# First token chunk of an attention and SwiGLU kernel: scores of both head groups for its first half ahead, first two wide products by halves of 256 tokens

## The chip, the cores and the metric

The kernel runs on one core of one Trainium2 chip. The metric is device time in microseconds (us) of that core, the median over several executions. Every kernel was timed in turn with the kernel before on the same chip. All profiled executions were of the undisturbed (fast) state, so fast runs are compared with fast runs throughout.

## The reference

Attention with projected keys and values (8 batches, 8 heads, 1024 tokens, head dimension 64; keys and values are projected from 1024 tokens to 64 by E and F), followed by a SwiGLU feed-forward network on the 8192 tokens of width 512, with an inner width of 1536:

```python
k_proj = np.einsum('ks,bhsd->bhkd', E, k)
v_proj = np.einsum('ks,bhsd->bhkd', F, v)
scores = scale * np.matmul(q, k_proj.transpose(0, 1, 3, 2))
scores = scores - np.max(scores, axis=-1, keepdims=True)
attn = np.exp(scores)
attn = attn / (np.sum(attn, axis=-1, keepdims=True) + 1e-09)
x = np.matmul(attn, v_proj)            # then [b, h, s, d] -> [b*s, h*d]
# ...
g = x @ w_gate
silu = g * (1.0 / (1.0 + np.exp(-g)))
val = x @ w_val
out = silu * val @ w_out
```

## The kernel before

The kernel works through 16 chunks of 512 tokens (two to a batch). For each chunk and each of 12 feature tiles of 128 it runs a gate block (`f_g`: four products of 128x512, summed over d_model) and a value block (`f_v`). The attention of later batches and the output products are slipped between these blocks by hand. Only the first chunk has nothing to hide behind, and all of this case is about it. Its attention is cut in four blocks `u`: head group `g` (heads 0-3 or 4-7) and token half `i` (256 tokens), with `g, i = divmod(u, 2)`. So `u` = 0, 1 is group 0, both halves, and `u` = 2, 3 is group 1.

The steps of a block, cut to their cores:

```python
def u_T(b, u, at, eng):   # transposes the queries of the block: 4 transposes, one copy (qT)
def u_S(b, u, at):        # scores: 4 products with BD (projected keys), Exp on ScalarE -> ee
def u_R(b, u):            # VectorE: row sums (zz) and reciprocal (rr)
def u_N(b, u):            # normalization, ee * rr -> AA
    # ...
    eng = nc.vector if b == 0 and u in (1, 3) else nc.gpsimd
def u_A(b, u, eng):       # 4 transposes of AA into a bank of the pool ps_a (3 banks), copy -> AT
def u_PV(b, ch, pr, eng): # one product of 512 tokens for a pair of heads, copy -> xT
def u_KV(b, what, hs, at):# projection of the keys or values of heads hs: 8 products (256 columns);
                          # for values, two copies into BDV:
    # ...
            eng = nc.vector if b or h0 else nc.scalar

def f_g(c, f):
    ps = ps_g.tile([P, CW], FP32, name="gps", tag="gps")      # ps_g has 2 banks
    x = xT[divmod(c, CH)]
    for kt in range(NKT):
        nc.tensor.matmul(out=ps[:], lhsT=wg[:, kt, f * P : (f + 1) * P], rhs=x[:, kt, :],
                         start=(kt == 0), stop=(kt == NKT - 1))
    th = fw.tile([P, CW], FP32, name="th", tag="th")
    nc.scalar.activation(out=th[:], in_=ps[:], func=AF.Tanh, scale=0.5)
    gp[0] = (ps, th)
```

The order of the opening; `warm(n)` issues n products of zeros (fillers) that are meant to keep the matrix engine's clock up:

```python
        warm(8)
        turn(0)
        turn(1)
        warm(6)
        u_KV(0, "k", (0, 4), at="y")
        # ... warm, key transposes, the other key half, warm ...
        u_T(0, 0, "a", nc.scalar)
        u_T(0, 1, "a", nc.scalar)
        warm(2)
        u_S(0, 0, "g")
        u_S(0, 1, "g")
        u_T(0, 2, "a", nc.scalar)
        u_T(0, 3, "a", nc.scalar)
        u_R(0, 0); u_N(0, 0); u_R(0, 1); u_N(0, 1)     # four lines in the kernel
        load_w_gv(4, 6, (0,))
        warm(3)
        u_S(0, 2, "g")
        u_S(0, 3, "g")
        for u in (2, 3):
            u_R(0, u)
            u_N(0, u)
        # ... loads ...
        warm(3)
        u_A(0, 0, nc.scalar)
        u_KV(0, "v", (0, 4), at="y")
        u_A(0, 1, nc.scalar)
        u_PV(0, 0, 0, nc.vector)
        u_PV(0, 0, 1, nc.vector)
        warm(3)
        u_A(0, 2, nc.scalar)
        u_KV(0, "v", (4, 8), at="y")
        u_A(0, 3, nc.scalar)
        u_PV(0, 0, 2, nc.scalar)
        u_PV(0, 0, 3, nc.vector)
        # ... then the stream: f_g, f_v of each feature tile ...
```

The softmax here doesn't subtract the row's maximum and nothing guards it: scores larger than these inputs give would overflow.

Of the kernel before, what the change touches and what calls it, by code (L numbers as in the profile page):

```python
# [12 lines left out]
BF16 = mybir.dt.bfloat16  # L13
# [9 lines left out]
P = 128  # L23
NJ = S // P
NPAIR = H // 2
NKT = DM // P
# [8 lines left out]
def kernel(  # L35
# [98 lines left out]
    def copy(eng, out, in_):  # L134
        (nc.scalar.copy if eng is nc.scalar else eng.tensor_copy)(out=out, in_=in_)  # L135

    def u_KV(b, what="kv", hs=(0, H), at="a"):
# [20 lines left out]
        if "v" in what:  # L158
            tv = t[64:128].rearrange("p (a c) d -> p a c d", c=2)
            ps = slice(h0 // 2, h1 // 2)  # L160
            eng = nc.vector if b or h0 else nc.scalar
            copy(eng, BDV[b % 2][0:64, ps, 0:64], tv[:, ps, 0, :])
            copy(eng, BDV[b % 2][64:128, ps, 64:128], tv[:, ps, 1, :])
# [83 lines left out]
    def u_N(b, u):  # L247
# [6 lines left out]
        else:  # L254
            a = AA[b, u] = aw.tile([P, 2, 4, KP], BF16, name="AA", tag="AA", bufs=4)
            a = a[:]
        eng = nc.vector if b == 0 and u in (1, 3) else nc.gpsimd
        eng.tensor_tensor(  # L258
# [22 lines left out]
    def u_PV(b, ch, pr, eng=nc.scalar):  # L281
# [10 lines left out]
        copy(eng, xT[b, ch][:, pr, :], ps[:])  # L292


    gp = {}

    def f_g(c, f):
        ps = ps_g.tile([P, CW], FP32, name="gps", tag="gps")
        x = xT[divmod(c, CH)]
        for kt in range(NKT):  # L300
            nc.tensor.matmul(  # L301
                out=ps[:],
                lhsT=wg[:, kt, f * P : (f + 1) * P],
                rhs=x[:, kt, :],
                start=(kt == 0),
                stop=(kt == NKT - 1),
            )
        th = fw.tile([P, CW], FP32, name="th", tag="th")
        nc.scalar.activation(out=th[:], in_=ps[:], func=AF.Tanh, scale=0.5)  # L309
        gp[0] = (ps, th)  # L310

    def f_v(c, f):
        ps = ps_v.tile([P, CW], FP32, name="vps", tag="vps")
        x = xT[divmod(c, CH)]
        for kt in range(NKT):
            nc.tensor.matmul(  # L316
                out=ps[:],
                lhsT=wv[:, kt, f * P : (f + 1) * P],
                rhs=x[:, kt, :],
                start=(kt == 0),  # L320
                stop=(kt == NKT - 1),
            )
        g, th = gp.pop(0)
# [74 lines left out]
    with tc.manual_schedule():  # L398
# [45 lines left out]
        turn(1)  # L444
        warm(6)
        u_KV(0, "k", (0, 4), at="y")
        warm(2)
        u_KT(0, at="v", prs=(0, 2))
        warm(3)
        u_KV(0, "k", (4, 8), at="y")  # L450
        warm(2)
        u_KT(0, at="v", prs=(2, 4))
        u_T(0, 0, "a", nc.scalar)
        u_T(0, 1, "a", nc.scalar)
        warm(2)
        u_S(0, 0, "g")
        u_S(0, 1, "g")
        u_T(0, 2, "a", nc.scalar)
        u_T(0, 3, "a", nc.scalar)
        u_R(0, 0)  # L460
        u_N(0, 0)
        u_R(0, 1)
        u_N(0, 1)
        load_w_gv(4, 6, (0,))
        warm(3)
        u_S(0, 2, "g")
        u_S(0, 3, "g")
        for u in (2, 3):
            u_R(0, u)
            u_N(0, u)  # L470
        load_w_gv(4, 6, (1,))
# [6 lines left out]
        load_k(1)  # L478
        warm(3)
        u_A(0, 0, nc.scalar)  # L480
        u_KV(0, "v", (0, 4), at="y")
        u_A(0, 1, nc.scalar)
        u_PV(0, 0, 0, nc.vector)
        u_PV(0, 0, 1, nc.vector)
        warm(3)
        u_A(0, 2, nc.scalar)
        u_KV(0, "v", (4, 8), at="y")
        u_A(0, 3, nc.scalar)
        u_PV(0, 0, 2, nc.scalar)
        u_PV(0, 0, 3, nc.vector)  # L490

# [32 lines left out]
        for t in range(NIT):  # L524
            c, f = divmod(t, NFT)
            f_g(c, f)
            run_slot(2 * t)
            f_v(c, f)
            for a in ypart.pop(t, ()):
                f_y(*a)  # L530
            run_slot(2 * t + 1)
# [32 lines left out]
```

## Time and profile before

| | before |
|---|---|
| time, median of 3 (lowest to highest) | 582.17 us (581.18 to 582.97) |
| span of the profiled execution | 580.9 us |
| matrix engine busy | 98% of the span |
| first wide product (gate block of f=0) | starts at 25.08 us |
| gate block of f=2 | starts at 28.82 us |
| from there to the end | 552.1 us |

How to read it. The matrix engine is busy nearly all the time and makes up nearly the whole chain that ended last. A change of the order at the start can therefore win only what it lets the stream of wide products start earlier. The right place to read is one fixed event in that stream. From the gate block of f=2 on, both kernels have the same instructions on the matrix engine in the same order, so its start is the measure. In the matrix engine's timeline of the kernel before (start, length, engine, line, operation, out<-in, shapes, count) it is this line:

```profile
28.82 1.03 PE L301 MATMUL gps<-xT,wg 128*128 128x512 bf16 x4
```

Span less this start, 580.9 - 28.82, is the 552.1 us that a change at the start has to leave alone. The other lines of the opening are in the prediction below.

### The profile page before, as it was taken

Reading aid. Unit: us, or ns where it says so; the run is one execution under the profiler, and the core shown is the slowest. Engines: PE = TensorE matmul, PEld = TensorE weight load, DVE = VectorE, ACT = ScalarE, POOL = GpSimd, SP = SyncE. Lnnn points to the kernel's source line nnn. Section 1 sums busy time; section 2 is a strip of 40 time slices with the busy share of each in tenths; the row PEclk is TensorE's granted clock in tenths of the full one; section 3 lists DMA queues with packets and bytes.
Section 4 is the critical chain, followed back from the end, with each engine's and each line's share of the span. In section 5 each row is a group of like instructions: output and inputs, shape, how many; then the busy total and the mean of one; then the engine's idle time right before and its main releaser. Section 6 shows DMA issues by size and latency. Waiting matters only on the chain.

```text
span 580.9 us, 7889 instructions
## 1 busy us (share of the span) xinstructions
PE 567.5 (98%) x2918; PEld 268.1 (46%) x2976; DVE 340.8 (59%) x588; ACT 237.4 (41%) x415; POOL 108.1 (19%) x121
## 2 busy tenths in 40 slices
PE   8899999999999999999999999999999999999997
PEld 4444444544444444444444444444444444444443
DVE  2677565766556754666546764566646675545550
ACT  1644435454435434354344434354343543443321
POOL 6715030224102320025001240022300220000000
PEclk8999999999999999999999999999999999999999
DMA  9999954209951499016970299303991122001002
GB/s 160 195 202 180 213 80 96 73 20 173 165 115 37 88 184 183 35 50 111 176 156 36 55 155 195 69 36 77 195 181 38 41 52 72 37 36 37 24 32 90
DMA packets 101623, 60.29 MB, mean 104 GB/s; under 512 B 53840, under 2 KB 93264, under 8 KB 101584
## 3 DMA queue, kind: packets, MB, share of 16 engines
q0 software_dynamic: 42288, 29.89, 35.6%
q1 hardware_dynamic: 59296, 29.89, 23.4%
q8 instruction: 23, 0.38, 0.3%
q14 instruction: 16, 0.13, 0.1%
HBM read 60.29 MB, written 16.78 MB: 133 GB/s over the span
## 4 chain that ended last, share of the span: by engine, by line
PE 94%; ACT 2%; DVE 2%; issue 1%; DMA 1%; DVEq 0%; ACTq 0%
PE yps L342 28%; PE vps L316 28%; PE gps L301 27%; PE kvp L147 3%; PE sc L227 2%; PE pv L285 2%; PE warm L430 1%; DMA Eraw<-in_E_dram 1%; ACT qT L135 1%; DVE hT L330 1%; PE aTp L274 0%; PE qTp L193 0%; PE kTp L172 0%; DVE s L325 0%; ACT ee L231 0%
## 5 line engine op out<-in xcount | busy, mean ns | idle before, releaser
L325 DVE SCALAR_TENSOR_TENSOR s<-th,gps 128x512 f32<-128x512 f32 x192 | 130.6, 680 | 134.2 <-ACT th L309 134.0
L301 PE MATMUL gps<-xT,wg 128*128 128x512 bf16 x750 | 195.8, 379 | 1.3 <-ACT xT L135 0.3
L316 PE MATMUL vps<-xT,wv 128*128 128x512 bf16 x751 | 195.3, 379 | 1.0 <-issue 0.2
L342 PE MATMUL yps<-wo,hT 128*128 128x512 bf16 x747 | 191.7, 379 | 1.7 <-ACT ysb L351 0.7
L309 ACT ACTIVATE th<-gps 128x512 f32<-128x512 f32 x192 | 114.7, 597 | 165.9 <-PE gps L301 156.7
L330 DVE TENSOR_TENSOR hT<-s,vps 128x512 bf16<-128x512 f32 x192 | 132.0, 688 | 22.7 <-PE vps L316 3.2
L342 PEld LDWEIGHTS <-hT 128*128 128x128 bf16 x768 | 75.1, 98 | 91.5 <-issue 1.0
L316 PEld LDWEIGHTS <-wv 128*128 128x128 bf16 x768 | 72.9, 98 | 83.4 <-issue 4.0
L301 PEld LDWEIGHTS <-wg 128*128 128x128 bf16 x768 | 73.1, 98 | 81.9 <-issue 1.0
L258 POOL TENSOR_TENSOR AAd<-ee,rr 128x512 bf16<-128x512 f32 x48 | 50.0, 1041 | 300.5 <-issue 165.8
L351 ACT ACTIVATE ysb<-yps 128x512 f32<-128x512 f32 x64 | 38.2, 597 | 79.3 <-PE yps L342 75.9
L135 ACT CAST xT<-pv 128x512 bf16<-128x512 f32 x61 | 35.4, 585 | 50.8 <-PE pv L285 50.8
L242 DVE TENSOR_REDUCE zz<-ee 128x8 f32<-128x512 f32 x64 | 43.5, 680 | 21.3 <-ACT ee L231 21.1
L231 ACT ACTIVATE ee<-sc 128x512 f32<-128x512 f32 x64 | 37.9, 596 | 20.7 <-PE sc L227 20.6
L258 POOL TENSOR_TENSOR AA<-ee,rr 128x512 bf16<-128x512 f32 x14 | 14.5, 1041 | 62.8 <-DVE rr L244 45.7
L285 PE MATMUL pv<-AT,BDV 128*128 128x512 bf16 x64 | 23.6, 379 | 1.8 <-ACT AT L135 1.6
L135 DVE CAST BDV<-kvp 64x256 bf16<-64x256 f32 (+1 forms) x16 | 6.6, 410 | 23.0 <-ACT ks L157 20.0
L227 PEld LDWEIGHTS <-qTd 128*128 128x128 bf16 x192 | 14.8, 98 | 11.3
L227 PE MATMUL sc<-BD,qTd 128*128 128x128 bf16 x192 | 18.6, 219 | 0.1
L244 DVE RECIPROCAL rr<-zz 128x8 f32<-128x8 f32 x64 | 13.0, 203 | 6.6 <-DVE zz L242 0.5
L147 PE MATMUL kvp<-kb,ET 128*64 128x512 bf16 (+1 forms) x72 | 16.2, 371 | 0.0
L147 PE MATMUL kvp<-vb,FT 128*64 128x512 bf16 (+1 forms) x72 | 15.5, 358 | 0.0
(46 smaller groups left out, 159.0 us busy)
## 6 DMA issues: line engine op xcount, KB each, us to landing
out_dram<-ysb SPq DMA_DIRECT2D x64, 256.0 KB, 2.3
qb<-in_q_dram POOLq DMA_DIRECT2D x15, 512.0 KB, 17.7
kb<-in_k_dram POOLq DMA_DIRECT2D x7, 1024.0 KB, 11.1
vb<-in_v_dram POOLq DMA_DIRECT2D x7, 1024.0 KB, 13.7
wo<-in_moe_w_out_dram POOLq DMA_DIRECT2D x2, 768.0 KB, 15.6
wg<-in_moe_w_gate_dram POOLq DMA_DIRECT2D x5, 256.0 KB, 10.6
wv<-in_moe_w_val_dram POOLq DMA_DIRECT2D x5, 256.0 KB, 10.6
kb<-in_k_dram POOLq DMA_DIRECT2D x2, 512.0 KB, 8.2
```

The source lines that it names most:

```text
L135: (nc.scalar.copy if eng is nc.scalar else eng.tensor_copy)(out=out, in_=in_)
L147: nc.tensor.matmul(out=t[lo : lo + 64, h0:h1].rearrange("p h d -> p (h d)"), lhsT=w[:, j, :], rhs=src[b][:, h0:h1, j, :], start=(j == 0), ...
L227: nc.tensor.matmul(out=ps[:, n, :], lhsT=t[:, n, :], rhs=BD[b % 2][:, 4 * g + n, :], start=True, stop=True)
L242: nc.vector.reduce_sum(out=z[:], in_=e[:], axis=AX.X)
L258: eng.tensor_tensor(out=a.rearrange("p j h k -> p h j k"), in0=ee.pop((b, u))[:], in1=rr.pop((b, u))[:].unsqueeze(3).to_broadcast([P, 4, 2 ...
L301: nc.tensor.matmul(out=ps[:], lhsT=wg[:, kt, f * P : (f + 1) * P], rhs=x[:, kt, :], start=(kt == 0), stop=(kt == NKT - 1),)
L309: nc.scalar.activation(out=th[:], in_=ps[:], func=AF.Tanh, scale=0.5)
L316: nc.tensor.matmul(out=ps[:], lhsT=wv[:, kt, f * P : (f + 1) * P], rhs=x[:, kt, :], start=(kt == 0), stop=(kt == NKT - 1),)
L325: nc.vector.scalar_tensor_tensor(out=s1[:], in0=th[:], scalar=1.0, in1=g[:], op0=ALU.add, op1=ALU.mult)
L330: nc.vector.tensor_tensor(out=hT[c][:, f, :], in0=s1[:], in1=ps[:], op=ALU.mult)
L342: nc.tensor.matmul(out=yy[c][:], lhsT=hT[c][:, f, i * P : (i + 1) * P], rhs=wo[:, f, :], start=(f == 0), stop=(f == NFT - 1),)
L351: nc.scalar.activation(out=ysb[:], in_=yy.pop(c)[:], func=AF.Copy, scale=0.5)
```

## The change

The intent is to get wide products going on the first 256 tokens while the attention of the other 256 is still being made. It does this in five ways:
1. The four blocks come as 0, 2, 1, 3: both head groups of token half 0 first. The normalizations on VectorE become blocks 2 and 3 (second of each pair, as before).
2. The attention products run by token half (`u_PV2`: two products of 256 columns into one bank, one copy).
3. The gate and value blocks of f=0 and f=1 run by halves of 256 tokens: the first halves as soon as half 0 is there, the second halves in the loop.
4. The value projections move ahead of the attention products. The BDV copies of heads 4-7 go to ScalarE.
5. Fewer fillers: after the opening eight, 15 in place of 24.

Some copies and banks move along with these (see the diff).

```diff
-            eng = nc.vector if b or h0 else nc.scalar
+            eng = nc.vector if b else nc.scalar
...
-        eng = nc.vector if b == 0 and u in (1, 3) else nc.gpsimd
+        eng = nc.vector if b == 0 and u in (2, 3) else nc.gpsimd
...
+    def u_PV2(b, ch, g, i, eng):
+        ...
+        ps = ps_a.tile([P, 2, CW // 2], FP32, name="pv", tag="pa")
+        for n in range(2):
+            nc.tensor.matmul(
+                out=ps[:, n].rearrange("p (j t) -> p j t", t=P),
+                lhsT=BDV[b % 2][:, 2 * g + n, :],
+                rhs=AT[b, ch][:, 2 * i : 2 * i + 2, 2 * g + n, :],
+                start=True, stop=True,
+            )
+        copy(eng, xT[b, ch][:, 2 * g : 2 * g + 2, 256 * i : 256 * (i + 1)], ps[:])
...
+    def f_mm(c, f, w, i=None):
+        if i != 1:
+            half[c, f, w] = bank("gv"[w], [P, CW], FP32, "gv"[w] + "ps")
+        ps = half[c, f, w]
+        ts = slice(0, CW) if i is None else slice(256 * i, 256 * (i + 1))
+        ... four products of ps[:, ts], as f_g had them for ps[:]
...
-        warm(6)
+        warm(7)
...
-        u_T(0, 1, "a", nc.scalar)
-        warm(2)
+        u_T(0, 1, "a", nc.vector)
+        u_T(0, 2, "a", nc.scalar)
         u_S(0, 0, "g")
-        u_S(0, 1, "g")
-        u_T(0, 2, "a", nc.scalar)
-        u_T(0, 3, "a", nc.scalar)
+        u_T(0, 3, "v", nc.vector)
+        u_S(0, 2, "g")
+        u_S(0, 1, "a")
+        u_S(0, 3, "a")
         u_R(0, 0)
         u_N(0, 0)
+        u_R(0, 2)
+        u_N(0, 2)
+        load_w_gv(4, 6, (0,))
+        u_KV(0, "v", (0, 4), at="y")
+        warm(1)
+        u_A(0, 0, nc.scalar)
         u_R(0, 1)
         u_N(0, 1)
...
+        u_R(0, 3)
+        u_N(0, 3)
+        u_A(0, 2, nc.scalar)
+        u_KV(0, "v", (4, 8), at="y")
...
+        warm(1)
+        u_PV2(0, 0, 0, 0, nc.scalar)
+        u_PV2(0, 0, 1, 0, nc.vector)
         u_A(0, 1, nc.scalar)
...
+        u_A(0, 3, nc.vector)
+        f_mm(0, 0, 0, 0)
+        f_mm(0, 0, 1, 0)
+        u_PV2(0, 0, 0, 1, nc.scalar)
+        u_PV2(0, 0, 1, 1, nc.vector)
+        f_mm(0, 1, 0, 0)
+        f_mm(0, 1, 1, 0)
...
-            f_g(c, f)
+            i = 1 if t < 2 else None
+            f_g(c, f, i)
```

More of the change, by code (lines that the diff above doesn't have):

```diff
@@ L292, in u_PV @@
         copy(eng, xT[b, ch][:, pr, :], ps[:])
-    gp = {}
-    def f_g(c, f):
-        ps = ps_g.tile([P, CW], FP32, name="gps", tag="gps")
+    def u_PV2(b, ch, g, i, eng):
+        if (b, ch) not in xT:
+            xT[b, ch] = x_pool.tile([P, NPAIR, CW], BF16, name="xT", tag=f"xT{ch}")
+        ps = ps_a.tile([P, 2, CW // 2], FP32, name="pv", tag="pa")
[4 more added lines that the diff above has]
+                rhs=AT[b, ch][:, 2 * i : 2 * i + 2, 2 * g + n, :],
+                start=True,
+                stop=True,
+            )
+        copy(eng, xT[b, ch][:, 2 * g : 2 * g + 2, 256 * i : 256 * (i + 1)], ps[:])
+    gp = {}
+    half = {}
+    def f_mm(c, f, w, i=None):
+        if i != 1:
+            half[c, f, w] = bank("gv"[w], [P, CW], FP32, "gv"[w] + "ps")
+        ps = half[c, f, w]
         x = xT[divmod(c, CH)]
+        ts = slice(0, CW) if i is None else slice(256 * i, 256 * (i + 1))
         for kt in range(NKT):
             nc.tensor.matmul(
-                out=ps[:],
-                lhsT=wg[:, kt, f * P : (f + 1) * P],
-                rhs=x[:, kt, :],
+                out=ps[:, ts],
+                lhsT=(wg, wv)[w][:, kt, f * P : (f + 1) * P],
+                rhs=x[:, kt, ts],
                 start=(kt == 0),
@@ L307, in f_g @@
             )
+        return ps
+    def f_g(c, f, i=None):
+        ps = f_mm(c, f, 0, i)
         th = fw.tile([P, CW], FP32, name="th", tag="th")
@@ L310, in f_g, with f_v @@
         gp[0] = (ps, th)
-    def f_v(c, f):
-        ps = ps_v.tile([P, CW], FP32, name="vps", tag="vps")
-        x = xT[divmod(c, CH)]
-        for kt in range(NKT):
-            nc.tensor.matmul(
-                out=ps[:],
-                lhsT=wv[:, kt, f * P : (f + 1) * P],
-                rhs=x[:, kt, :],
-                start=(kt == 0),
-                stop=(kt == NKT - 1),
-            )
+    def f_v(c, f, i=None):
+        ps = f_mm(c, f, 1, i)
         g, th = gp.pop(0)
@@ L448 @@
         u_KT(0, at="v", prs=(0, 2))
-        warm(3)
+        warm(2)
         u_KV(0, "k", (4, 8), at="y")
@@ L453 @@
         u_T(0, 0, "a", nc.scalar)
-        u_T(0, 1, "a", nc.scalar)
-        warm(2)
+        u_T(0, 1, "a", nc.vector)
+        u_T(0, 2, "a", nc.scalar)
         u_S(0, 0, "g")
-        u_S(0, 1, "g")
-        u_T(0, 2, "a", nc.scalar)
-        u_T(0, 3, "a", nc.scalar)
+        u_T(0, 3, "v", nc.vector)
+        u_S(0, 2, "g")
+        u_S(0, 1, "a")
+        u_S(0, 3, "a")
         u_R(0, 0)
         u_N(0, 0)
+        u_R(0, 2)
[4 more added lines that the diff above has]
+        u_A(0, 0, nc.scalar)
         u_R(0, 1)
         u_N(0, 1)
-        load_w_gv(4, 6, (0,))
-        warm(3)
-        u_S(0, 2, "g")
-        u_S(0, 3, "g")
-        for u in (2, 3):
-            u_R(0, u)
-            u_N(0, u)
+        u_R(0, 3)
+        u_N(0, 3)
+        u_A(0, 2, nc.scalar)
+        u_KV(0, "v", (4, 8), at="y")
         load_w_gv(4, 6, (1,))
@@ L478 @@
         load_k(1)
-        warm(3)
-        u_A(0, 0, nc.scalar)
-        u_KV(0, "v", (0, 4), at="y")
+        warm(1)
+        u_PV2(0, 0, 0, 0, nc.scalar)
+        u_PV2(0, 0, 1, 0, nc.vector)
         u_A(0, 1, nc.scalar)
-        u_PV(0, 0, 0, nc.vector)
-        u_PV(0, 0, 1, nc.vector)
-        warm(3)
-        u_A(0, 2, nc.scalar)
-        u_KV(0, "v", (4, 8), at="y")
-        u_A(0, 3, nc.scalar)
-        u_PV(0, 0, 2, nc.scalar)
-        u_PV(0, 0, 3, nc.vector)
+        u_A(0, 3, nc.vector)
[5 more added lines that the diff above has]
+        f_mm(0, 1, 1, 0)
         for i, u in enumerate(range(4, 8)):
@@ L525 @@
             c, f = divmod(t, NFT)
-            f_g(c, f)
+            i = 1 if t < 2 else None
+            f_g(c, f, i)
             run_slot(2 * t)
-            f_v(c, f)
+            f_v(c, f, i)
             for a in ypart.pop(t, ()):
```

## The prediction

> **What bounds the kernel now.** I read the page's busy shares first, then its chain of work that ended last, then the order of work on each engine over the first 30 us, and last the transfers issued there with their times to landing.
>
> From the page, busy shares and slices of 14.5 us:
>
> ```profile
> PE 567.5 (98%) x2918; PEld 268.1 (46%) x2976; DVE 340.8 (59%) x588; ACT 237.4 (41%) x415; POOL 108.1 (19%) x121
> ...
> PE   8899999999999999999999999999999999999997
> ...
> PEclk8999999999999999999999999999999999999999
> ...
> PE 94%; ACT 2%; DVE 2%; issue 1%; DMA 1%; DVEq 0%; ACTq 0%
> ```
>
> The matrix engine is at 98% and is 94% of the chain that ended last. Only the first two slices are visibly under-filled, and only in the first is the granted clock low. So the end comes when the steady stream of wide products ends, and a change to the start is worth as many microseconds as the stream begins earlier, no more.
>
> The matrix engine's timeline, just before the stream (start, length, operation):
>
> ```profile
> 15.15 0.89 PE L227 MATMUL sc<-BD,qT 128*128 128x128 bf16 x8
> 15.88 0.61 PE L193 MATMUL qTp<-ident_bf,qb 128*128 128x128 bf16 x8
> 16.32 0.81 PE L430 MATMUL warm<-zeros 128*128 128x512 bf16 x3
> 17.21 0.89 PE L227 MATMUL sc<-BD,qT 128*128 128x128 bf16 x8
> 17.93 0.81 PE L430 MATMUL warm<-zeros 128*128 128x512 bf16 x3
> 18.58 0.39 PE L274 MATMUL aTp<-ident_bf,AA 128*128 128x128 bf16 x4
> 18.89 1.06 PE L147 MATMUL kvp<-vb,FT 128*64 128x256 bf16 x8
> ...
> 21.19 0.59 PE L285 MATMUL pv<-AT,BDV 128*128 128x512 bf16 x2 [0.90 <-ACT AT L135]
> ...
> 22.58 1.06 PE L147 MATMUL kvp<-vb,FT 128*64 128x256 bf16 x8
> ...
> 24.65 0.59 PE L285 MATMUL pv<-AT,BDV 128*128 128x512 bf16 x2 [0.67 <-ACT AT L135]
> 25.08 1.32 PE L301 MATMUL gps<-xT,wg 128*128 128x512 bf16 x4
> ```
>
> The first useful wide product starts at 25.08; before it stand fillers (warm) and waits on small copies. From there a gate block and a value block of four products each alternate every 0.86 us, so the third feature tile (f=2) starts its gate block at 28.82.
>
> What feeds it is VectorE's softmax chain, whose lines are back to back:
>
> ```profile
> 16.22 0.69 DVE L242 TENSOR_REDUCE zz<-ee 128x8 f32<-128x512 f32 x1 [1.10 <-ACT ee L231]
> ...
> 17.97 0.92 DVE L258 TENSOR_TENSOR AA<-ee,rr 128x512 bf16<-128x512 f32 x1
> ...
> 20.55 0.92 DVE L258 TENSOR_TENSOR AA<-ee,rr 128x512 bf16<-128x512 f32 x1
> ```
>
> Its two normalizations end at 18.89 and 21.47; GpSimd's two (1.04 us each, started at 17.30 and 19.88) end at 18.34 and 20.92. The four blocks thus come as 18.34, 18.89, 20.92, 21.47. Today the first pair is head group 0, both token halves; nothing wide can run until the second pair is in, as a wide product sums over all heads.
>
> [...] (0.86 us for four of 512 columns, 0.215 each), so I estimate 0.109 us for 256 columns: halving a wide product costs nothing in stream time. [...] the fillers before 9 us take 0.40 us each (2.39 us for six), and a window of 8 to 10 us reads a clock of 0.50. [...] VectorE's AT copy (128x512 bf16) takes 0.42 us and the fp32 xT copy 0.69. [...] The trace's bank wait of that kind is yps behind the ysb copy, 0.69 us near the end.
>
> **The change part by part.** The compiled order of the two kernels shows that from the gate block of f=2 on, the matrix engine's instructions are the same in kind and order. So all is decided before that point, which was 28.82.
>
> Until 14 us: a seventh cold filler adds 0.4 us before the first key projection, but that projection (eight products at 0.21 cold) then runs more of its time under the risen clock, and one filler (0.215) less stands before the second projection. I take the net as 0 ± 0.2, so the second BD part still starts at 13.92.
>
> Scores: twelve query transposes at 0.055 run 14.08 to 14.74 (the query's second part landed at 4.7 + 9.7 = 14.4). ScalarE copies two of the three to 15.58, VectorE the other after its BD copies (free at 15.11) in about 0.4. Scores 0, 2, 1, 3 leave the matrix engine at 15.4, 15.85, 16.1, 16.5, against 17.9 for the last before. The exponentials chain at 0.49 pitch from 15.59 to 17.7 instead of 18.7. This is 1 us of earliness, but the first reduce still begins at 16.22, and VectorE was already back to back. So the four normalizations end where they did. What changes is whose they are: 18.34 and 18.89 are now both head groups of token half 0.
>
> The value projections no longer stand between: part 0 starts when v heads 0-3 land, 5.5 + 11.5 = 17.0, and ends at 18.0. Transposes of the first pair: 18.4 and 18.95. Part 1 needs v heads 4-7, which landed at 6.2 + 13.3 = 19.5 (before, it ran at 22.58, long after). It runs 19.5 to 20.5; its two BDV copies, now on ScalarE at 0.27 each, end at 21.15. This landing, not the softmax, becomes the gate of half 0.
>
> Then, on the estimated 0.109: attention product of group 0 at 20.75, its xT copy on ScalarE behind the BDV copies, 21.15 to 21.75; group 1 at 21.2 to 21.45, its copy on VectorE 21.6 to 22.3 (0.69). The transpose of the last block needs a third bank of that pool, freed by the ScalarE copy at 21.75, so it runs at 21.8 to 22.0. The first half gate block runs 22.0 to 22.6, waiting on the VectorE copy in its middle; the half value block to 23.0. Attention products of half 1: 23.0 to 23.45; f=1's two half blocks: 23.45 to 24.3. The copies of half 1 end at 24.0 (ScalarE) and 24.35 (VectorE). The second halves of f=0 and f=1 follow: four blocks of 0.436, 24.35 to 26.1.
>
> f=2 then needs the bank of f=0's gate: tanh (0.60) after 24.95, then the 0.69 product on VectorE, free at about 26.35. So f=2 starts at 26.35 instead of 28.82: **2.45 us earlier**. Check by contents: removed are fillers (6+2+3+2+2+3+3+3 = 24 after the opening eight, now 7+2+2+2+1+1 = 15: nine, about 1.9 us) and the idle stretches (0.90 and 0.67 us marked above, with smaller ones); added are waits for v of perhaps 0.9.
>
> Weights: those of f=0 and f=1 landed at 20.2, 21.0, 21.7, 23.1; the half blocks that use them start at 22.0, 22.6, 23.45, 23.9. The next ones landed at 24.0 and 25.3 (needed 26.35 and 27.2) and 26.6 and 28.0 (needed 29.8 and 30.7). GpSimd's order of normalizations and transfers is unchanged, so they land as before. All fits, the tightest by 0.8 us.
>
> The median before is 582.17, so I predict **579.7 us**, 0.4% less.
>
> **The rivals.** First, a transfer takes the place of the removed wait: if v or the second value weights land 1 us later than in this one trace, the gain falls to about 1.5 us (580.7). For: the transfer engines are saturated in the first slices. Against: their order and issue times do not change. Second, small copies become the bound: ScalarE and VectorE get narrow copies one after another between 20.5 and 24.4, with three banks shared by transposes and attention products. If each of some five handovers costs 0.2 more than I counted, 1 us is lost. Third, banks: f=2 behind f=0's tanh and product; I count 0.25 us, it could be 0.6 if VectorE is late. Fourth, the clock: were the shorter filling to lose it, eight products would cost 0.43 each and the gain would go (582 or above). The matrix engine was busy only 1.04 of 2 us in 20 to 22 before with the clock at 1.00, so I think it unlikely. For more than 2.45: if v lands earlier, half 0 is gated by 18.89 instead and another 0.5 us is won (579.2). All are small beside 2%, 11.6 us, because nothing after 28.82 changes; later blocks wait on transfers issued relative to the stream, and the next keys landed at 51.6 while needed at 62.4.
>
> **Range and chances.** The runs of before spread over 1.8 us, half of which is noise of the median; the rivals span 579.2 to 581.2 and noise widens that below. Range 578.3 to 581.3. A move over 2% either way would need a disturbance elsewhere: 0.01 faster, 0.98 same, 0.01 slower.
>
> **What would show it.** In the changed profile: the gate block of f=2 near 26.35; first half gate block near 22.0; the value projection of heads 4-7 starting at its landing, near 19.5, with a wait on that transfer; VectorE's first reduce still near 16.2 and its last normalization near 21.5; clock 1.00 from 11 us on; the stretch from f=2 to the end as long as before (580.9 - 28.8 = 552.1) to within 0.5. Wrong if the last is longer (the lead given back to a later wait), if the reduce starts later (the key projection slipped behind the seventh filler), or if half blocks are spaced by more than 0.11.

The forecast's sum is: f=2 at 26.35 us in place of 28.82, about 2.45 us earlier (2.47 by these two starts). Its 0.109 us for a product of 256 columns is the author's estimate. The trace of before alone gives the same, on a straight line between 0.056 us for 128 columns (eight query transposes in 0.61 us, of which one alone takes 0.22) and 0.215 for 512 (eight products from 27.10 to 28.82). That the transfer engines were saturated is read from the page of before: its DMA row shows 9 tenths or more in each of the first five slices, at 160 to 213 GB/s. The bank wait named there is a block of output products that waited 0.69 us, at 566.33 us, for ScalarE's copy out of the bank (ysb). That filling keeps the clock up, as the fourth rival has it, was an assumption; e8 and e9 test it.

## The result and the profile after

| | before | after |
|---|---|---|
| time, median (lowest to highest) | 581.67 us (581.1 to 582.97), 4 runs | 580.34 us (579.26 to 580.44), 4 runs |
| span of the profiled execution | 580.9 | 578.6 |
| gate block of f=2 starts | 28.82 | 26.80 |
| from there to the end | 552.1 | 551.8 |

The four runs of before are the three of the start and one beside the changed kernel. The ratio is 0.997 (95% interval 0.9948 to 0.9992): faster by 0.3%, well within the 2% band. A ratio here is the mean time of one kernel's fast runs over the mean of the other's of the same rounds, so not quite the ratio of the medians quoted.

From the page of the changed kernel, busy shares, granted clock in 40 slices, and shares of the chain that ended last:

```profile
PE 567.8 (98%) x2987; PEld 268.7 (46%) x2987; DVE 340.4 (59%) x588; ACT 236.8 (41%) x415; POOL 107.9 (19%) x121
...
PEclk9999999999999999999999999999999999999999
...
PE 93%; DMA 2%; DVE 2%; ACT 1%; POOL 1%; issue 0%; POOLq 0%; DVEq 0%; ACTq 0%
```

The matrix engine has as much to do as before (567.8 us against 567.5). What went is waiting and filling ahead of the stream. The timeline of the changed kernel's matrix engine (in brackets: the idle time just before, and what ended it):

```profile
17.41 1.03 PE L147 MATMUL kvp<-vb,FT 128*64 128x256 bf16 x8 [0.62 <-DMA vb<-in_v_dram]
...
19.97 1.06 PE L147 MATMUL kvp<-vb,FT 128*64 128x256 bf16 x8 [0.42 <-DMA vb<-in_v_dram]
...
22.48 0.72 PE L322 MATMUL gps<-xT,wg 128*128 128x256 bf16 x4
...
24.79 0.60 PE L322 MATMUL gps<-xT,wg 128*128 128x256 bf16 x4
25.23 0.60 PE L322 MATMUL vps<-xT,wv 128*128 128x256 bf16 x4
...
26.80 1.02 PE L322 MATMUL gps<-xT,wg 128*128 128x512 bf16 x4
```

Before, the waits marked ahead of the wide products were for copies on ScalarE. Now the second value projection stands 0.42 us waiting for its transfer, and the first half gate block runs at 22.48, against 25.08 for the first full block before. Half blocks come 0.44 us apart (24.79, 25.23; six of them from 23.92 to 26.10, so 0.436), four products in each, so a product of 256 columns costs 0.109 us. Two halves take 0.87 us where a full block takes 0.86: halving costs the stream next to nothing. The chain that ended last, in order of time (start, length, what):

```profile
6.18 13.75 DMA vb<-in_v_dram
...
19.97 1.07 PE kvp L147 x8
```

The value transfer, issued at 6.18 us, is now in the chain: it landed at 6.18 + 13.75 = 19.93. VectorE's last normalization has hardly moved:

```profile
20.75 0.92 DVE L258 TENSOR_TENSOR AA<-ee,rr 128x512 bf16<-128x512 f32 x1
```

It ends at 21.67, against 21.47 before. It was not the gate before either. The chain that ended last in the kernel before runs at this place through the matrix engine's own queue:

```profile
21.83 0.59 PE warm L430 x2
...
22.65 0.99 PE kvp L147 x8
23.64 0.34 PE aTp L274 x4
```

The transposes (`aTp`) of the last normalization began at 23.58, 2.1 us after it had ended: fillers and the second value projection stood ahead of them. From 14.5 us to f=0's first gate block this chain holds no instruction of VectorE, in either trace of before (this one and e7).

Of the 2.3 us by which the span is shorter, 2.02 lie before f=2. Span less start (551.8) is 0.3 us shorter than before; the cause of that is open.

### The profile page after: what moved, and what is told of

Its sections match the earlier page's. It is cut to its first block, busy times and chain, and to the rows that moved or that the text cites. A ratio compares the mean times of both kernels' runs of the same rounds, so it can differ in the third digit from the quotient of the medians.

```text
span 578.6 us, 7968 instructions
## 1 busy us (share of the span) xinstructions
PE 567.8 (98%) x2987; PEld 268.7 (46%) x2987; DVE 340.4 (59%) x588; ACT 236.8 (41%) x415; POOL 107.9 (19%) x121
## 4 chain that ended last, share of the span: by engine, by line
PE 93%; DMA 2%; DVE 2%; ACT 1%; POOL 1%; issue 0%; POOLq 0%; DVEq 0%; ACTq 0%
PE yps L358 29%; PE vps L322 28%; PE gps L322 28%; PE kvp L147 3%; DMA vb<-in_v_dram 2%; PE sc L227 2%; PE pv L285 2%; DVE hT L346 1%; DVE s L341 0%; PE aTp L274 0%; DVE zz L242 0%; ACT ysb L367 0%; PE qTp L193 0%; ACT qT L135 0%; POOL kb L88 0%
## 5 line engine op out<-in xcount | busy, mean ns | idle before, releaser
L322 PE MATMUL gps<-xT,wg 128*128 128x512 bf16 (+1 forms) x776 | 198.1, 377 | 0.5 <-ACT xT L135 0.3
L322 PE MATMUL vps<-xT,wv 128*128 128x512 bf16 (+1 forms) x776 | 197.5, 377 | 0.0
L358 PE MATMUL yps<-wo,hT 128*128 128x512 bf16 x768 | 194.6, 379 | 0.7 <-ACT ysb L367 0.7
L258 POOL TENSOR_TENSOR AA<-ee,rr 128x512 bf16<-128x512 f32 x14 | 14.5, 1040 | 59.0 <-DVE rr L244 21.9
L285 PE MATMUL pv<-AT,BDV 128*128 128x512 bf16 x60 | 22.4, 379 | 0.2 <-DVE AT L135 0.2
L135 DVE CAST BDV<-kvp 64x256 bf16<-64x256 f32 x14 | 6.0, 427 | 22.1 <-ACT ks L157 20.0
```

The lines of the kernel that those rows point to most:

```text
L135: (nc.scalar.copy if eng is nc.scalar else eng.tensor_copy)(out=out, in_=in_)
L258: eng.tensor_tensor(out=a.rearrange("p j h k -> p h j k"), in0=ee.pop((b, u))[:], in1=rr.pop((b, u))[:].unsqueeze(3).to_broadcast([P, 4, 2 ...
L322: nc.tensor.matmul(out=ps[:, ts], lhsT=(wg, wv)[w][:, kt, f * P : (f + 1) * P], rhs=x[:, kt, ts], start=(kt == 0), stop=(kt == NKT - 1),)
L358: nc.tensor.matmul(out=yy[c][:], lhsT=hT[c][:, f, i * P : (i + 1) * P], rhs=wo[:, f, :], start=(f == 0), stop=(f == NFT - 1),)
```

## The experiments

Twelve runs were made. The profile is one execution of each. The times are medians, and each ratio is to the runs of before.

| run | what it is | time, us | ratio to before | f=2 starts | span - f=2 |
|---|---|---|---|---|---|
| e0 | the change again | 579.85 | 0.9962 | 26.68 | 551.8 |
| e1 | the change, full-width first blocks | 580.39 | 0.9971 | 27.21 | 551.9 |
| e2 | the change, blocks in the old order | 580.67 | 0.9979 | 27.28 | 551.8 |
| e3 | the change, no wait for v of heads 4-7 (wrong result) | 579.76 | 0.996 | 26.52 | 551.8 |
| e4 | the change, last v part split in two | 579.43 | 0.9958 | 25.65 | 551.9 |
| e5 | before, with the change's late fillers | 581.85 | 0.9988 | 28.10 | 552.1 |
| e6 | e5, value projection ahead | 581.7 | 0.9988 | 28.52 | 551.8 |
| e7 | before, unaltered | 582.74 | 1.0011 | 28.66 | 552.0 |
| e8 | the change, 3 opening fillers for 7 | 580.21 | 0.9959 | 25.49 | 551.8 |
| e9 | the change, no fillers after the first eight | 580.51 | 0.9961 | 26.44 | 551.9 |
| e10 | the change, value projection before the second transposes | 580.34 | 0.9961 | 27.41 | 551.8 |
| e11 | e4, first normalization on VectorE too | 580.08 | 0.9957 | 26.55 | 551.8 |

The intervals are about ±0.0013 to ±0.0018 wide, that is 0.8 to 1 us, so times alone separate the change from before, but hardly the variants from one another. The last column is what makes single traces usable: over all kernels the part after f=2 is 551.8 to 552.1 us. An earlier f=2 thus reaches the end of the traced execution whole, and differences of its start within one trace, from a fixed event to f=2, carry the argument. The theory at this point was that of the prediction: half 0 is gated by the landing of v, and the gain is the sum of the halves, the order and the fillers. The rivals were that fillers alone did it, and that the softmax chain is still the gate.

### e0: the change again

No edit; it measures the noise between two traces of one kernel.

> The changed kernel once more, unaltered, to size its gain better than four runs did. Theory 'landing' (the start of the wide stream is gated by the transfer of v heads 4-7, which varies from run to run): gain of 1.5 to 2.5 us; in the trace, the gate block of f=2 starts 6.9 us (plus or minus 0.2) after v heads 4-7 land, wherever that landing lies between 19.3 and 20.2. Rival 'copies' (the small copies and banks set the start, at fixed times): f=2 starts at 26.8 whatever the landing is.

Measured: 579.85 us, ratio 0.9962 (0.9949 to 0.9975), f=2 at 26.68. From the matrix engine's timeline:

```profile
6.42 1.10 PE L434 MATMUL efp<-ident_fp,Fraw 64*128 64x64 f32 x8 [0.79 <-DMA Fraw<-in_F_dram]
7.56 3.14 PE L446 MATMUL warm<-zeros 128*128 128x512 bf16 x7
...
12.89 1.06 PE L147 MATMUL kvp<-kb,ET 128*64 128x256 bf16 x8
...
19.85 1.06 PE L147 MATMUL kvp<-vb,FT 128*64 128x256 bf16 x8
```

The seven fillers took 3.14 us here and 1.67 us in the first trace of the same kernel, where the clock was up already. Here they stood in the key chain. They also began late, at 7.56 against 7.06, because the transposes of F ahead of them waited 0.79 us for its transfer. The second key projection began at 12.89, against 12.21 in that trace and 12.39 before. The first reduce on VectorE came at 16.73 (16.43, and 16.22 before). Yet f=2 came 0.12 us earlier than in the first trace, as the value projection did (19.85 against 19.97). From its start to f=2 both traces have the same 6.83 us. So a key chain 0.3 to 0.7 us later cost the stream nothing: the projection began right behind the transposes of half 0, just as v landed (13.6 us after its issue at 6.18, so near 19.8). This run alone does not tell the theory from its rival, as f=2 came 6.9 us after the landing and also within 0.12 us of 26.8. That f=2 does not come at a fixed time is shown by e4 and e8 (25.65 and 25.49).

### e1: full-width first blocks

```diff
-        f_mm(0, 0, 0, 0)
-        f_mm(0, 0, 1, 0)
         u_PV2(0, 0, 0, 1, nc.scalar)
         u_PV2(0, 0, 1, 1, nc.vector)
-        f_mm(0, 1, 0, 0)
-        f_mm(0, 1, 1, 0)
...
-            i = 1 if t < 2 else None
+            i = None
```

> The reordering alone: attention products still by token halves, but all wide products at full width, so the first can start only when the xT copies of half 1 are done. Theory: the halving of the wide products carries most of the gain, since it fills about 1.75 us (four half blocks of 0.436) that would otherwise wait. First gate block near 24.8, f=2 at 24.8 + 4 x 0.8625 = 28.3, so 1.5 us slower than the change, only about 0.5 faster than before. Rival: the reordering carries the gain, and this is within 0.5 us of the change.

Measured: 580.39 us, ratio 0.9971 (0.9957 to 0.9985), f=2 at 27.21. The matrix engine's timeline:

```profile
22.71 0.60 PE L300 MATMUL pv<-AT,BDV 128*128 128x256 bf16 x4 [0.30 <-ACT AT L135]
...
23.77 1.02 PE L322 MATMUL gps<-xT,wg 128*128 128x512 bf16 x4 [0.45 <-ACT xT L135]
```

The value projection began at 19.74, so 7.47 us passed to f=2 in place of 6.83: the halves are worth 0.64 us, not 1.5. Without half blocks ahead of them, the attention products of half 1 run at 22.71 rather than at 23.48 (their start in the changed kernel), so the first full block comes at 23.77. The expectation had left the products of half 1 where they were.

### e2: blocks in the old order

The blocks come as 0, 1, 2, 3 again, VectorE normalizes 1 and 3, and half 0 needs blocks 0 and 2; the halves, `u_PV2` and the fillers stay as in the change.

```diff
-        u_S(0, 2, "g")
-        u_S(0, 1, "a")
+        u_S(0, 1, "g")
+        u_S(0, 2, "a")
...
-        u_A(0, 2, nc.scalar)
+        u_A(0, 1, nc.scalar)
         u_KV(0, "v", (4, 8), at="y")
+        u_A(0, 2, nc.scalar)
```

> The halving kept, but scores and normalizations in the old order (both halves of head group 0, then of group 1), so half 0 is complete only with the third normalization, near 21.0 instead of 19.1; its transpose stands after the second value projection. Theory 'landing': the landing of v heads 4-7 hides most of these 1.9 us; first half gate block ends about 0.5 us later, f=2 at about 27.3, the kernel 0.4 to 0.7 us slower than the change. Rival 'softmax is the gate': 1.5 to 2 us slower, the whole gain gone.

Measured: 580.67 us, ratio 0.9979 (0.9961 to 0.9997; one of its runs took 582.8), f=2 at 27.28. The matrix engine's timeline:

```profile
22.15 0.38 PE L300 MATMUL pv<-AT,BDV 128*128 128x256 bf16 x2 [0.25 <-ACT AT L135]
...
23.31 0.38 PE L322 MATMUL gps<-xT,wg 128*128 128x256 bf16 x2 [0.29 <-DVE xT L135]
```

The value projection began at 19.86, so f=2 came 7.42 us after it, 0.59 more than with the new order (0.5 was expected). Half 0's second head group is now in the second pair of normalizations. Its product waits for the copy of its transposes. The first half gate block begins at 22.64 (22.48 in the change), but its last two products wait for an xT copy until 23.31.

### e3: no wait for v of heads 4-7

The second value projection reads the values of heads 0-3, which landed earlier. The result is wrong on purpose (relative error 0.39); the work is the same.

```diff
-                    rhs=src[b][:, h0:h1, j, :],
+                    rhs=src[b][:, 0:4, j, :] if (b, what, h0) == (0, "v", 4) else src[b][:, h0:h1, j, :],
```

> Wrong result on purpose: the second value projection reads v heads 0-3, which are already there, so it no longer waits for heads 4-7; all transfers are still made. Theory 'landing': the projection starts near 19.4 instead of 19.97, the BDV copies end near 21.0, then VectorE's last normalization (ends near 21.7) becomes the gate for the copy of group 1; f=2 at about 26.4, 0.3 to 0.6 us faster than the change. Rival 'copies': no change at all, as VectorE and the banks set the start anyway.

Measured: 579.76 us, ratio 0.996 (0.9946 to 0.9973), f=2 at 26.52. The matrix engine's timeline:

```profile
19.36 0.40 PE L274 MATMUL aTp<-ident_bf,AA 128*128 128x128 bf16 x4 [0.15 <-DVE AA L258]
19.69 1.06 PE L147 MATMUL kvp<-vb,FT 128*64 128x256 bf16 x8
```

The wait is gone, and almost nothing was won by the medians: 0.1 us (e0: 579.85), far inside the interval. The trace can't size the wait either. v landed early in it (12.6 us after its issue, so at 18.8, and was not waited for anyway), and the key chain was late, as in e0 (second key projection at 12.80). So the transposes of half 0, which stand ahead of the projection, began only at 19.36 behind VectorE's normalization. What it shows is the next gate: with v out of the way the softmax of half 0 holds the start. In the first trace of the change that gate stood 0.42 us ahead of v, which bounds what taking the wait away would have won there.

### e4: last v part in two transfers

```diff
-        load_v(0, (0, 4, 8))
+        load_v(0, (0, 4, 6, 8))
...
-        u_KV(0, "v", (4, 8), at="y")
+        u_KV(0, "v", (4, 6), at="y")
+        u_KV(0, "v", (6, 8), at="v")
```

> The change, and v heads 4-7 loaded and projected as two parts of two heads (the last part into a bank of its own, so that it needn't wait for the copies out of the first): only 8 products of 128 columns (about 0.45 us, not 1.0) follow the last landing. Theory 'landing': f=2 0.3 to 0.4 us earlier relative to the landing, at about 26.4, the kernel 0.3 faster than the change. Rival 'VectorE': its last normalization (ends near 21.7) holds the copy of group 1, gain under 0.2.

Measured: 579.43 us, ratio 0.9958 (0.9945 to 0.9971), f=2 at 25.65; not told apart from the change by time. The clock was up early in this trace (seven fillers in 1.67 us), keys and values landed early (v near 18.5), and the matrix engine did not wait for v of heads 4-7. So whether the split helps when v is late was not tested. The sixteen products of 128 columns took 1.08 us together, so about 0.5 for the eight of the last part (half of it, an estimate; 0.45 was expected). In VectorE's and GpSimd's timeline:

```profile
16.61 1.85 DVE L258 TENSOR_TENSOR AA<-ee,rr 128x512 bf16<-128x512 f32 x1
16.84 1.05 POOL L258 TENSOR_TENSOR AA<-ee,rr 128x512 bf16<-128x512 f32 x1
```

VectorE's normalization took twice its 0.92 us. It held the transposes of half 0, and behind them the value projection (18.84). In every trace before this one it began 0.66 us after GpSimd's and so lay beside its last 0.37 us alone; here it began 0.23 us before it and lay beside all of it. Experiment e11 takes this up.

### e5: before, with the change's late fillers

In the kernel before, the fillers after the second key projection go from 2, 3, 3, 3 to 0, 0, 1, 1 (the two right behind that projection stay):

```diff
-        warm(2)
         u_S(0, 0, "g")
...
-        warm(3)
         u_S(0, 2, "g")
...
-        warm(3)
+        warm(1)
         u_A(0, 0, nc.scalar)
...
-        warm(3)
+        warm(1)
         u_A(0, 2, nc.scalar)
```

> The kernel before with only its fillers after the second key projection cut (2, 3, 3, 3 become 0, 0, 1, 1); order and widths unchanged. Theory 'fillers on the path': three of them stood between the first attention products and the third transpose and held back the second value projection (22.58), though its data had landed near 19.5; f=2 starts at about 28.0 to 28.2 instead of 28.8, 0.6 to 0.8 us faster than before. Rival 'fillers only fill waits': same time as before; second rival: the granted clock falls and it is slower.

Measured: 581.85 us, ratio 0.9988 (0.9972 to 1.0003), f=2 at 28.10:

```profile
28.10 1.03 PE L301 MATMUL gps<-xT,wg 128*128 128x512 bf16 x4
```

The last normalization ends at 21.34 here, so 6.76 us pass to f=2, where the two traces of before have 7.35 and 7.36: 0.59 us is what these nine fillers cost, as expected (0.6 to 0.8). That event is not on the path; a count from one that is, the second key projection, gives 0.60 (15.83 us to f=2, against 16.43 and 16.44). The times alone do not tell e5 from before. They are about a quarter to a third of the gain, so the rival "only the fillers" falls.

### e6: before, fewer fillers, value projection ahead

```diff
         u_A(0, 1, nc.scalar)
+        u_KV(0, "v", (4, 8), at="y")
         u_PV(0, 0, 0, nc.vector)
...
         u_A(0, 2, nc.scalar)
-        u_KV(0, "v", (4, 8), at="y")
```

Its BDV copies go to ScalarE as in the change; all else is e5.

> As the run with fewer fillers, and the second value projection (its BDV copies on ScalarE) put ahead of the attention products, where its data has just landed; scores in the old order, every wide product at full width. Theory 'position of the value projection': this alone moves f=2 to 26.9 to 27.3, 1.5 to 2 us faster than before and within 0.5 us of the change. Rival 'token halves carry it' (my prediction's account): f=2 near 28.0, no better than fewer fillers alone.

Measured: 581.7 us, ratio 0.9988 (0.9973 to 1.0003), f=2 at 28.52, which is 6.87 us after the last normalization (e5: 6.76). Nothing was won; the expectation missed. The matrix engine's timeline shows why:

```profile
23.28 0.38 PE L274 MATMUL aTp<-ident_bf,AA 128*128 128x128 bf16 x4 [0.67 <-DVE xT L135]
```

With the value projection out of the way the last transposes stand idle for 0.67 us until a bank of the three-bank pool is free, and it is held by the xT copies on VectorE. These began at 21.99, 0.34 us after the last normalization, when the attention products behind the value projection were done. Moved alone, part 4 of the change only moves the wait; with products by token half and one xT copy on ScalarE (parts 2 and 4 together) that wait is gone.

### e7: the kernel before again

> The kernel before, unaltered, for a second trace and to size noise. Its eleven earlier runs fall into two groups, near 581.1 and near 582.6. Theory 'clock phase': in the lower group the clock rose before the first key projection, so that the keys' part ends 0.5 to 0.9 us sooner and the whole stream with it; if this trace is of the lower group its clock reads 1.00 from 8 us on and f=2 starts near 27.5; of the upper, 28.8 again. The ratio should be 1.000 within 0.001.

Measured: 582.74 us, ratio 1.0011 (0.9996 to 1.0027), f=2 at 28.66, 7.36 us after the last normalization (21.30). The ratio is just outside the expected 0.001. In this trace the clock had risen by the first key projection (1.10 us, against 1.75 in the first trace), and yet f=2 came only 0.16 us earlier, as the six fillers ahead of it had run cold (2.72 us). Over the four calls and this run, 12 of the 48 runs of before took 581.0 to 581.6 us, 34 took 582.0 to 583.2 and two 584.1 and 585.2. These two groups, near 581.2 and near 582.6, do not overlap. Those of e5 and e6 fall apart likewise (near 580.5 and 581.9). Both traces of before (spans 580.9 and 580.7) are of the upper group, so what sets the lower one was not seen. The clock is not excluded: the eleven of the 48 runs with a mean clock of 0.997 are all in the upper group; but that group has runs at 0.999 and 1.000 too. The changed kernel and its variants did not split so visibly. Against the lower group the change wins about 1 us, against the upper one about 2.5.

### e8 and e9: three opening fillers, and none

```diff
-        warm(7)
+        warm(3)
```

For e9 every `warm` after the first `warm(8)` is taken out.

> The change with 3 fillers instead of 7 ahead of the first key projection. In traces where the clock was still low there (0.40 to 0.43 us a filler), the projection started at 9.7 though k had landed near 8.0 to 9.4. Theory 'the opening fillers hold the key chain in a low clock': the projection starts at k's landing or near 8.3, the normalizations end up to 0.5 us sooner, f=2 at 26.0 to 26.5 unless v lands late; 0.2 to 0.5 us faster than the change. Rival 'the fillers buy the clock': with fewer of them the clock rises later, the keys' products run at half speed, same or slower than the change.

Measured, e8: 580.21 us, ratio 0.9959 (0.994 to 0.9977), f=2 at 25.49. In its trace the key projection began at 8.49 and ran cold (1.86 us for eight), everything followed 1.2 to 1.4 us earlier than in e0 (0.43 of it was there before the fillers began, at 7.13 against 7.56), and v landed early too (its projection began at 18.66, 6.83 us ahead of f=2). The timed runs do not show the gain: within noise of the change.

> The change with every filler after the opening eight removed. Theory: the matrix engine is then busy well under half of the time from 7 to 20 us, the granted clock is low or falls again in that stretch, key and value projections take 1.7 us instead of 0.9 to 1.0, and the kernel is 0.5 to 2 us slower than the change. Rival 'fillers are not needed': within 0.3 us of the change or faster.

Measured, e9: 580.51 us, ratio 0.9961 (0.9944 to 0.9979), f=2 at 26.44. The matrix engine's timeline, and below it one row of the stretches (us; busy time and instructions of the matrix engine, its weight load, VectorE, ScalarE, GpSimd; granted clock; DMA share; GB/s):

```profile
9.30 1.86 PE L147 MATMUL kvp<-kb,ET 128*64 128x256 bf16 x8 [2.27 <-DMA kb<-in_k_dram]
```

```profile
10.00:12.00 2.00, 1.54 (x9) 0.88 (x8) 0.06 (x1) 0.37 (x1) 0.29 (x1) 1.00 1.39 195
```

Both key projections ran cold (1.86 and 1.69 us, where 1.03 to 1.06 is the warm length), and the value projection still began at its landing (19.61), so it cost nothing: the expected loss of 0.5 to 2 us did not come. The clock column reads 1.00 in a stretch in which the products run at half rate. That is no reading of the clock: the kept trace holds no clock event (an entry that says what clock is granted from then on) before 13.2 us, and the column shows 1.00 where it has none. There the spacing of the products is to be believed. The fillers left in the change are not needed for this gain.

### e10: value projection before the second transposes

```diff
+        u_KV(0, "v", (4, 8), at="y")
         u_A(0, 2, nc.scalar)
-        u_KV(0, "v", (4, 8), at="y")
```

> The change with the second value projection ahead of the transpose of group 1 instead of behind it. In all traces of this order f=2 came 6.8 us after that projection began, and it began either at v's landing (19.7 to 20.0) or behind that transpose (19.4 to 19.6). Theory: where v lands early (before 18.9) this wins up to 0.4 us, where it lands late (19.8) the transpose and its copy now come 1 us later and it loses 0.3 to 0.6; on average 0.2 us slower than the change. Rival 'landing alone gates': no loss in late landings, a gain in early ones.

Measured: 580.34 us, ratio 0.9961 (0.9943 to 0.9978), f=2 at 27.41:

```profile
19.99 1.06 PE L147 MATMUL kvp<-vb,FT 128*64 128x256 bf16 x8 [0.95 <-DMA vb<-in_v_dram]
20.98 0.40 PE L274 MATMUL aTp<-ident_bf,AA 128*128 128x128 bf16 x4
```

v landed late, and the transposes, which were ready, stood behind it on the same queue: from the projection to f=2 it took 7.42 us, 0.59 more than with the transposes first. The change has the better order when v is late. The times cannot tell the two apart.

### e11: no GpSimd normalization beside VectorE's in the first pair

```diff
-        eng = nc.vector if b == 0 and u in (2, 3) else nc.gpsimd
+        eng = nc.vector if b == 0 and u in (0, 2, 3) else nc.gpsimd
```

The rest is e4.

> The split-v kernel with one more edit: the first normalization (group 0, token half 0) runs on VectorE too, so the first pair has no GpSimd normalization beside it; the second pair stays split between GpSimd and VectorE as a control. In every trace so far VectorE's normalization took 0.92 us when it began 0.66 after GpSimd's (so beside its last 0.37 us), and 1.85 in the one trace where it began before GpSimd's and lay beside all 1.05 of it. Theory A, the two engines hold each other up: alone, VectorE's normalization takes about 0.92 - 0.37 = 0.55 us (between 0.5 and 0.65), both of the first pair, while the control, beginning 0.66 after GpSimd's, is 0.92 again. Theory B, 0.92 is the operation's own length and the 1.85 was something else: both take 0.92. On the time: under A the first pair ends about 0.55 + 0.63 + 0.15 + 0.55 = 1.9 after the first reciprocal, about as in the change (0.12 + 0.63 + 0.2 + 0.92), so f=2 starts as in the split-v trace or up to 0.6 earlier (25.0 to 25.7 if v lands by 18.5); under B the pair ends 0.4 to 0.7 later and half 0 is held by it: f=2 at 25.7 to 26.5. One more effect: GpSimd issues the next gate weights about 1 us earlier, behind v in the queue; if that delays v's last part, it lands after 19.5. Time within noise of the split-v kernel (579.4 +- 0.7) either way.

Measured: 580.08 us, ratio 0.9957 (0.9944 to 0.9971), f=2 at 26.55. VectorE's and GpSimd's timeline:

```profile
17.10 0.69 DVE L258 TENSOR_TENSOR AA<-ee,rr 128x512 bf16<-128x512 f32 x1
...
18.66 0.69 DVE L258 TENSOR_TENSOR AA<-ee,rr 128x512 bf16<-128x512 f32 x1
...
20.34 1.04 POOL L258 TENSOR_TENSOR AA<-ee,rr 128x512 bf16<-128x512 f32 x1 [0.94 <-DVE rr L244]
...
21.01 0.92 DVE L258 TENSOR_TENSOR AA<-ee,rr 128x512 bf16<-128x512 f32 x1
```

Alone the normalization takes 0.69 us, both times. The control, which began 0.67 us after GpSimd's, takes 0.92 again. So neither theory's number holds (0.55 and 0.92), but the direction of A does: beside 0.37 us of GpSimd's normalization VectorE loses 0.23 us, and in e4, beside all 1.05 us, it lost 1.85 - 0.69 = 1.16 (one trace). GpSimd's own length, 1.03 to 1.05 us, is the same in every trace. So in these traces VectorE's operation is held up beside GpSimd's and GpSimd's is not; by what mechanism was not shown. Which of the two began first does not settle it: in e4 VectorE began 0.23 us first by the profile and yet took 1.85 us (one trace, and starts on GpSimd are rough). For the kernel it is a poor trade. With both on VectorE the first pair ends 2.49 us after the first reciprocal begins (16.86 to 19.35), against 1.94 in the changed kernel (17.15 to 19.09), and the transposes hold the value projection at 19.73.

No variant beats the change clearly: those with a lower median lie within its noise.

## Why the prediction was right

The prediction was 579.7 us, range 578.3 to 581.3, with 0.98 for a time within 2%. The changed kernel took 580.34 us in its first runs and 579.85 in the second. The range says little by itself, as its upper end takes in part of before's own faster group (581.0 to 581.6). The traces say more. Step by step:

- **That only the start matters** was right and is shown: over all kernels the part from f=2 on is 551.8 to 552.1 us (within the 0.5 it named), so nothing was given back later.
- **"What feeds it is VectorE's softmax chain"** was a misreading. In the chain that ended last of both traces of before, no VectorE instruction stands between 14.5 and 25 us. It runs through the matrix engine's queue, fillers among it, and ScalarE's copies. The last normalization (21.47) had 2.1 us to spare before its transposes began (23.58). Also, the page shows an under-filled slice at the end (7) besides the first two; the change does not touch it.
- **The chain of small steps from the value projection to f=2** was right as a sum: 19.5 to 26.35 makes 6.85 us, and 6.83 was measured in five traces of kernels that keep the change's order (after, e0, e3, e8, e9). In it the half blocks (0.109 us a product) and the bank of f=0's gate (0.26 against 0.25) came as worked out. The first half gate block was at 22.48 for 22.0; by far the most of that is the next point.
- **The landing of v** was mis-sized by 0.43 us. The step took 13.3 us from the trace of before; it was 13.75, and over the traces of unsplit v it is 12.2 to 13.8. That is the whole miss in that trace: f=2 at 26.80 for 26.35, and the first rival in small. The prediction's "its order and issue times do not change" is right, and is no warrant for the same landing.
- **"This landing, not the softmax"** was right in most traces and said too firmly. Of the seven traces of the unsplit v in which the projection has this wait, six show it: after, e1 and e2 by 0.41 to 0.42 us, e8 and e9 by 0.19, e10 by 0.95. In e0 it began right behind the transposes. Without the wait (e3) the times did not move by more than noise, because the transposes of half 0 stand 0.2 to 0.4 us ahead of the landing. Two gates within half a microsecond: that v's landing sets the start in a given trace is read from the marked wait; that removing it would win was expected, and is not shown.
- **The seventh filler as "0 ± 0.2"** held where traces can be compared. With cold fillers begun at 7.10 us, the second key projection came 5.00 and 5.03 us later with seven of them (e1, e2) and 5.12 and 5.17 with six (e7, e5); the clock rose at 9.5 to 9.9 us in these four. In e0 it came at 12.89 (before: 12.39) because F landed late and the fillers began at 7.56 instead of 6.93; from their start it is 5.33 us against 5.46. The sign that the prediction named, a later first reduce, did show (16.43 and 16.73 for 16.22), but not by the filler: in the first trace the query transposes waited 0.39 us for the query's second part, in e0 F came late. The later reduce cost the stream nothing, as v landed no earlier than the chain was done. With v out of the way (e3) fillers are the largest part of the first 30 us of the chain that ended last (27.8%, the opening eight included). In the trace after, the clock was up (seven fillers in 1.67 us) and the fillers cost nothing, and e8 and e9 show that fewer are no worse.
- **The cold fillers.** The prediction took them for a clock that had not yet risen. By the clock events in the trace of before it had risen at 3.9 us, fell to half at 7.3 and rose again at 10.7. The fillers' length (0.40 us) was read rightly. The first rise differs from trace to trace of this opening, though products begin at 1.19 to 1.20 us wherever the timeline was read from the start: by the clock events it comes anywhere from 3.9 us (before, e0, e11) to 10.5 (e3), and at 13.2 without fillers (e9). In e0 and e11 the clock falls and rises again as in before. The spacing of the fillers agrees (seven in 1.67 us in after, in 3.14 in e0).
- **The sum of parts.** The prediction did not divide its 2.45 us. The experiments do, each from a fixed event of the same trace: halves 0.64 (e1, from the value projection), order 0.59 (e2, likewise), late fillers 0.59 (e5, from the last normalization). They add up to 1.82, against 2.02 and 2.14 for the traces of the change and its repeat. As the events differ from experiment to experiment, the sum is a check of size and no exact account. The nine late fillers are 1.9 us by contents, as the prediction counted, but took only 0.59 us from the path. Counted from the second key projection, f=2 comes after 16.43 and 16.44 us in the traces of before, 14.59 in after and 13.79 in e0. So the change shortens what follows the keys by 2.64 us where v does not hold it (e0), but by 1.84 where it does (after). That the value projection moved ahead wins nothing by itself is shown by e6.
- **Chances.** Nothing came near 2% (11.6 us). The rival of a lost clock fell: even without fillers (e9) the part from f=2 on took 551.9 us, as in the others.

Open are the two groups of the kernel before, 1.4 us apart, and with them whether the gain is 1 us or 2.5 against a given run; the 0.2 to 0.3 us by which span less f=2 is shorter in the changed kernels and in e6; and what sets the landing of v within its 1.6 us.

## What to carry to other kernels

When the main engine is busy to 98%, measure a change of the start by one fixed instruction in the steady stream, and check that the remainder of the span is constant. Then single traces tell what a few timed rounds cannot. Order the first work so that the first slice of the stream needs the fewest inputs (here both head groups of half the tokens), but expect each removed wait to uncover another within half a microsecond: a landing, a bank, a copy. And count an operation's length with its neighbour in mind: an element-wise operation on VectorE that runs beside one on GpSimd can take more than twice as long as alone (1.85 us against 0.69 in one trace here).
